# Loads held back near the end of a range's attention, and sums on VectorE set behind the copies of turned q and k

## The chip, the cores and the metric

The kernel runs on 1 core of one Trainium2 chip. The metric is the device time of one execution in microseconds (us). The five engines are TensorE (PE in the profile; PEld is its loading of weights), VectorE (DVE), ScalarE (ACT), GpSimd (POOL) and SyncE (SP). Each works through its own instructions in the order in which the program gives them, and waits on semaphores for the others. DMAs are issued from the queues of SP, ACT and POOL.

## The reference

Softmax attention over 8 batches, 12 heads, 448 tokens and a head size of 64, then two products with a leaky ReLU between them:

```python
def _attn_ref(q, k, v):                       # (8, 12, 448, 64) each
    scores = matmul(q, k.transpose(0, 1, 3, 2)) / sqrt(64)
    attn = exp(scores - max(scores)); attn = attn / (sum(attn) + 1e-09)
    return matmul(attn, v)

x = attn_out.transpose(0, 2, 1, 3).reshape(3584, 768)
h = x @ w_in                                  # (768, 2048)
g = maximum(0.01 * h, h)
out = g @ w_out                               # (2048, 768), float32
```

## The kernel before

The attention is done in 48 units (8 batches, 6 pairs of heads). Of a unit, GpSimd loads q, k and v (L144, two units in one DMA) and casts them into order (L173 for q and k, L175 for v); q and k are turned, by TensorE and a copy on VectorE (L275) for the first fifteen units and by a DMA transpose on SP's queue (L252, `turn`) for the rest; TensorE computes four chunks of scores (L286); ScalarE takes their exp (L295); `rows` multiplies by v with 32 matmuls (L792) and VectorE divides by the row sums (L798, L799); x is turned into `xT`, by TensorE for a few units (L332, copied at L333) and by DMA transposes for the others. A v buffer (four of them) is free for the cast of unit u + 4 when the rows of unit u are done.

The 3584 tokens are cut into seven ranges (`cuts`), of 640, 512, ..., 384 and 512 tokens. Each range has a product with w_in (the hidden product) and a product over w_out, done as two blocks. The work of the units that the next range needs is laid between the matmuls of the current range. Range 0's hidden product is plain (`head` for the first 448 tokens, `neck` for the rest, L367 and L650). From range 1 on, the products use a scheme of seven block products instead of eight, Strassen's kind, which needs sums on VectorE: sums of x (`mix_x_part`, L431), of w_in (`mix_w_in`, L402 and L406), of w_out (`mix_weights`, L379 to L388) and of h (`mix_first`, L458 and L459, for range 0; `mix_h`, L451 and L452, for the others). In `hidden` (L486) the partial products are added by ScalarE copies (L498, L506, L510) and VectorE (L501, L513, L516); in `block_pair` (L558) by VectorE copies (L563) and joins (L566), and more sums of h (L570, L576).

The order on each engine is written out by hand and fixed when the program is built. A small planner decides it: `place` puts bursts of three score chunks, turns and rows between matmuls, by a model of time (`model["now"]`) that knows TensorE, ScalarE and the PSUM slots. `advance`, called every fourth step, adds at most one turn, one cast of q and k, one cast of v and, on every second call, one load of the tensor (q, k or v) that is furthest behind. What `advance` lets through depends on counters (`to["load"]`, `to["cast"]`, `to["turn"]`, `rows_done`, `chunk`), not on time on the chip. `second(i)` is the product of range i over w_out; in it the sums of x of range i + 1 are set when the planner's time is far enough past the rows that they need (`fresh`), and `summed` says for both parts whether all have been set. `need[i + 2]` is the number of units that range i + 1 needs.

`mix_weights` is a generator: each `next(outs)` puts its next sum in VectorE's queue (12 sums for the mixed weights, one empty step, four sums in place on the right half of w_out, L388). `neck` draws from it by the counts in `after`; what is left is drawn after `second(0)`. In `neck` the turn of the last unit that TensorE turns (`transposes(NPE - 1, ...)`) stands just ahead of the last draw. `early_sums` says after which group of `head` which pair of sums of h for range 0 is set; the second pair of token blocks has its sums set in two pieces, `known` (the 64 columns of `head`) and the rest in `second(0)`.

Of the kernel before, what the change touches and what calls it, by code (L numbers as in the profile page):

```python
# [16 lines left out]
def kernel(  # L17
# [13 lines left out]
    P = 128  # L31
    HP = H // 2
    SC = 112
    NSC = S // SC
# [7 lines left out]
    NR = len(cuts) - 1  # L42
    HEAD = S
    need = [HP * -(-t // S) for t in cuts]
# [24 lines left out]
    def next_slot():  # L69

        slots.append(slots.pop(0))
        return slots[-1]

    def next_bank():

        banks.reverse()
        return banks[1]
# [19 lines left out]
    def place_of(t):  # L97
        return (t + NX - cuts[3]) % NX
# [155 lines left out]
    def dma_transposes(u):  # L254
        if NPE <= u < NU:
            turn(qkT[u % NQ][:, :QL], qk_sb[u].rearrange("p i so h d -> p (i so h d)"))
# [5 lines left out]
    def transposes(u, bank=None):  # L262
        if u >= min(NPE, NU):
            return
        for parts in ((1,), (0,)) if u == 0 else ((0, 1),):
            tr = turn_tile(bank)
            for i in parts:
                for so in range(NSC):
                    nc.tensor.transpose(  # L269
                        tr[:, i, ts(so, SC)], qk_sb[u][:, i, so], ident[:SC, :SC]  # L270
                    )
            if u == 0:
                stay_warm(3 if parts == (1,) else 5)
            at = slice(parts[0], parts[-1] + 1)
            (nc.scalar.copy if u == 0 and parts == (1,) else nc.vector.tensor_copy)(  # L275
                qkT[u % NQ][:, :QL].rearrange("p (i s) -> p i s", i=2)[:, at], tr[:, at]
            )
# [73 lines left out]
    def settle(n=3):  # L351
        while late and n:
            expo(*late.pop(0))
            n -= 1
# [79 lines left out]
    def spots(i):  # L434

        if i == 0:
            return 0, [(0, 1), (2, 3)]
        return 0, [(0, 2), (1, 3)] if cuts[i + 1] - cuts[i] == 4 * P else [(0, 1), (KEEP, 2)]
# [15 lines left out]
    def mix_first(m, c, cols):  # L454

        one, two = (slice(x * P + cols.start, x * P + cols.stop) for x in spots(0)[1][c])
        lo, hi = slice(m, m + 2), slice(MH + m, MH + m + 2)
        nc.vector.tensor_sub(h_mix[:, lo, c, cols], h[:, lo, one], h[:, lo, two])  # L458
        nc.vector.tensor_add(h[:, lo, two], h[:, lo, two], h[:, hi, two])  # L459
# [150 lines left out]
        banks.reverse()  # L610

    known = slice(0, HEAD - 3 * P)
    early_sums = {9: (0, 0, slice(0, P)), 11: (2, 0, slice(0, P)), 12: (0, 1, known), 13: (4, 0, slice(0, P)), 14: (2, 1, known), 15: (6, 0, slice(0, P))}

    def head(ins):

# [20 lines left out]
    def neck(outs):  # L637

        n = cuts[1] - HEAD
        at = place_of(HEAD)  # L640
        ms = [x + y for x in range(0, MH, 2) for y in (0, MH)]
        held = {}

        def part2(m, kks):
            fresh = m not in held
            if fresh:
                held[m] = next_bank()
            for j in range(2):
                for kk in kks:
                    nc.tensor.matmul(  # L650
                        held[m][:, j * n:(j + 1) * n], w_in_sb[:, kk, ts(m + j, P)], xT[:, kk, at:at + n],
                        start=(fresh and j == 0 and kk == 0), stop=(kk == KD - 1), skip_group_check=True,
                    )

        assert all(u == need[1] - 1 for u, _ in owed_x), owed_x
        def after(x):
            for _ in range((0, 0, 2, 3, 4, 3, 3, 2)[x]):
                next(outs)

        for m in ms[:2]:  # L660
            part2(m, range(KD - 1))
        yield 4 * (KD - 1) * n / 2400, False
        for x, m in enumerate(ms):
            if x < 2:
                assert rows_done >= need[1], rows_done
                settle_x()
                part2(m, (KD - 1,))
                if x:
                    after(x - 1)
            else:  # L670
                part2(m, range(KH))
                after(x - 1)
                yield 2 * KH * n / 2400, False
                part2(m, range(KH, KD))
            nc.scalar.activation(
                h[:, m:m + 2, HEAD:cuts[1]], held.pop(m)[:, :2 * n].rearrange("p (m t) -> p m t", m=2), AX.Prelu, alpha=0.01
            )
            if x < 2:
                mix_first(4 + 2 * x, 1, known)
            settle(1)  # L680
            yield 2 * (KH if x > 1 else 1) * n / 2400, True
        model["free"][id(slots[0])] = model["now"] + 1.5
        transposes(NPE - 1, next_slot()[:, 0])
        after(len(ms) - 1)

    def supply(u):
# [69 lines left out]
    chunk = 4 * HP + 3  # L756
    rows_done = HP
    to = {"pe": HP + 2, "turn": NPE, "cast": HP + 4, "v": HP + 4, "load": [HP + 8] * 3}
    tick = 0

    def advance():
        nonlocal tick
        tick += 1
        u = to["turn"]
        if u < min(NU, chunk // NSC + NQ, to["cast"]):
            dma_transposes(u)
            to["turn"] += 1
        u = to["cast"]
        if u < min(NU, to["turn"] + 2, to["load"][0], to["load"][1]):
            cast(u, (0, 1))  # L770
            to["cast"] += 1
        u = to["v"]
        if u < min(NU, rows_done + NV, to["load"][2]):
            cast(u, (2,))
            to["v"] += 1
        if tick % 2 == 0:
            x = min(range(3), key=lambda x: to["load"][x])
            u = to["load"][x]
            if u < NU and u - 3 < (to["cast"], to["cast"], to["v"])[x]:
                load_soft(u, 2, (x,))  # L780
                to["load"][x] += 2
# [45 lines left out]
    def settle_x(now=None):  # L827
        while owed_x and (now is None or owed_x[0][1] <= now and model["free"].get(id(slots[0]), 0.0) <= now + 0.05):
            model["free"][id(slots[0])] = model["now"] + 1.0
            model["now"] += 0.3  # L830
            x_transposes(owed_x.pop(0)[0], next_slot()[:, 0])
# [102 lines left out]
    def second(i):  # L934

        x_sums = [mix_x_part(i + 1, slice(0, 2)), mix_x_part(i + 1, slice(2, 3))] if i + 1 < NR else []
        fresh, summed = [None, None], [i + 1 == NR] * 2
        left = plan[i]
        for c in range(len(spots(i)[1])):
            for x, _ in enumerate(block_pair(i, c)):  # L940
                if x % 4 == 0:
                    advance()
                if c or x:
                    model["now"] += 0.325
                left -= place(i, left, calm=x not in (1, 2), keen=need[min(i + 2, NR)], cap=NU if all(summed) else need[i + 2])
                if i == 0 and c == 0 and x in (5, 9, 13, 17):
                    mix_first((x - 5) // 2, 1, slice(HEAD - 3 * P, P))
                if i == 0 and c and x % 4 == 2:
                    next(ins, None)
                for y in range(2):  # L950
                    if fresh[y] is None and i + 1 < NR and rows_done >= need[i + 2] - 1 + y:
                        fresh[y] = model["now"] + (2.5 if need[i + 2] - 2 + y in X_PE else 7.0)
                for y, todo in enumerate(x_sums if x % 2 == 0 else ()):
                    if fresh[y] is not None and fresh[y] <= model["now"] and not summed[y] and not (y and owed_x):
                        summed[y] = next(todo, 0) is not None
                        if not summed[y]:
                            break
        assert left == 0 or chunk == NU * NSC, (i, left)
        assert i + 1 == NR or rows_done >= need[i + 2], (i, rows_done)
        settle_x()  # L960
        for todo in x_sums:
            for _ in todo:
                pass

    ins, outs = mix_w_in(), mix_weights()
# [16 lines left out]
    model["now"] += 0.45  # L982
    to["pe"] += 1
    second(0)
    for _ in ins:
        pass
    for _ in outs:
        pass
    for i in range(1, NR):
        for step, _ in enumerate(hidden(i)):  # L990
            advance()
            if step % 4 == 2 and NSC * (rows_done + 1) <= chunk:
                rows()
        model.update(now=0.0, act=2.3, free={id(x): 0.9 if cuts[i + 1] - cuts[i] == 4 * P and i + 1 < NR else 1.2 for x in slots}, ready={})
        second(i)
# [30 lines left out]
```

## Time and profile before

| what | us |
|---|---|
| three runs | 391.54, 389.33, 386.16 (median 389.33) |
| the profiled execution | 386.56 |
| its span, from the first to the last instruction | 384.8 |
| GpSimd idle ahead of casts of v (L175), until rows (L792) | 100.8, longest 17.8 |
| ScalarE idle ahead of exp (L295), until scores (L286) | 46.8, longest 2.7 |
| VectorE idle ahead of a sum of x (L431), until a DMA transpose of x | 3.3 in three waits, longest 2.3 |
| TensorE idle until a copy of turned q and k (L275), score matmuls alone | 1.2 in three waits |

The granted clock of TensorE is 1.0 throughout. A line of a timeline gives the start in us, the duration, the engine and line, the operation with what it writes and reads, how many instructions are merged in it, and in brackets the engine's idle time just before it with what ended that. Idle time of an engine that isn't the bottleneck costs nothing by itself.

### The profile page before, as it was taken

The page shows a single profiled execution, that of the slowest core. Times are in us where ns is not written, and L with a number is a line of the kernel's source. Part 1 is how long each engine was busy: PE and PEld are TensorE (multiplying, and loading weights), DVE is VectorE, ACT ScalarE, POOL GpSimd, SP SyncE. Part 2 cuts the span into 40 slices and gives each one's busy share as a digit, 9 for nine tenths or more (in the row PEclk, how much of TensorE's full clock was granted, in tenths as well). Part 3 has the DMA queues.
Part 4 walks back from the last instruction along what each step waited for, and adds up shares of the span by engine and source line. Part 5 has one row for each costly group of instructions (what it writes and reads, how often), then busy time and mean ns, then how long its engine had stood idle before and what let it go on. Part 6 is the DMA issues. An engine that isn't in the chain of part 4 may idle for free.

```text
span 384.8 us, 10038 instructions
## 1 busy us (share of the span) xinstructions
PE 374.4 (97%) x4091; PEld 258.6 (67%) x4091; DVE 236.4 (61%) x510; ACT 264.3 (69%) x391; POOL 142.5 (37%) x223
## 2 busy tenths in 40 slices
PE   7899999999999999899999999999999999999996
PEld 3665658656588655786568865678655795668854
DVE  3662887786756644757458674575745665474753
ACT  6997875856768777487776877667776777717700
POOL 5989684475735043530535305254051000000000
PEclk9999999999999999999999999999999999999999
DMA  7999999999999159991399942999329600421022
GB/s 156 168 202 203 181 192 208 176 139 169 159 183 149 26 101 174 166 135 26 54 204 140 133 69 50 198 137 168 48 50 165 152 18 2 108 66 42 3 80 85
DMA packets 92798, 46.98 MB, mean 122 GB/s; under 512 B 51408, under 2 KB 89424, under 8 KB 92752
## 3 DMA queue, kind: packets, MB, share of 16 engines
q0 software_dynamic: 37536, 22.24, 45.5%
q1 hardware_dynamic: 54576, 23.54, 33.2%
q8 instruction: 32, 0.52, 0.6%
q10 hardware_dynamic: 640, 0.56, 0.5%
q14 instruction: 14, 0.11, 0.1%
HBM read 45.61 MB, written 11.01 MB: 147 GB/s over the span
## 4 chain that ended last, share of the span: by engine, by line
PE 89%; DVE 4%; ACT 3%; DMA 3%; issue 1%; DVEq 0%; ACTq 0%
PE g L558 32%; PE g L486 14%; PE sc L486 14%; PE sc L792 10%; PE sc L286 10%; PE g L367 3%; ACT e L295 3%; PE g L650 2%; DMA xT<-x 2%; PE g L269 1%; DMA hmix<-in_k_dram 1%; DVE x L799 1%; PE g L305 1%; DVE qkT L275 1%; PE sc L367 1%
## 5 line engine op out<-in xcount | busy, mean ns | idle before, releaser
L295 ACT ACTIVATE e<-sc 112x896 bf16<-112x896 f32 x192 | 162.6, 920 | 46.9 <-PE sc L286 46.8
L558 PEld LDWEIGHTS <-h 128*128 128x128 bf16 x680 | 61.2, 97 | 47.8 <-issue 14.0
L558 PE MATMUL g<-w_out_sb,h 128*128 128x384 bf16 x448 | 87.2, 327 | 0.0
L175 POOL COPY v<-fv 112x512 bf16<-112x512 bf16 x38 | 26.1, 689 | 109.4 <-PE sc L792 100.8
L475 ACT ACTIVATE h<-c 128x512 bf16<-128x512 f32 (+1 forms) x72 | 43.5, 611 | 25.4 <-DVE c L501 16.4
L486 PEld LDWEIGHTS <-w_in_sb 128*128 128x128 bf16 x576 | 54.2, 98 | 7.5 <-issue 1.5
L286 PE MATMUL sc<-qkT 64*128 64x448 bf16 x384 | 50.5, 353 | 2.7 <-DVE qkT L275 1.2
L792 PEld LDWEIGHTS <-e 112*128 112x128 bf16 x1344 | 46.3, 97 | 5.2 <-ACT e L295 0.8
L792 PE MATMUL sc<-v,e 112*128 112x65 bf16 x1344 | 47.6, 193 | 0.6 <-ACT e L295 0.6
L486 PEld LDWEIGHTS <-w_in_mix 128*128 128x128 bf16 x432 | 41.1, 98 | 4.1
L563 DVE COPY o<-g 128x384 f32<-128x384 f32 x53 | 29.3, 553 | 22.6 <-PE g L558 22.4
L558 PE MATMUL g<-w_mix,h 128*128 128x384 bf16 (+1 forms) x224 | 41.6, 324 | 0.0
L286 PEld LDWEIGHTS <-qkT 64*128 64x128 bf16 x384 | 15.8, 94 | 30.6 <-issue 20.3
L173 POOL COPY qkb<-fq 112x512 bf16<-112x512 bf16 x38 | 25.2, 664 | 23.3 <-DMA fq<-in_q_dram 18.6
L173 POOL COPY qkb<-fk 112x512 bf16<-112x512 bf16 x38 | 25.5, 672 | 21.1 <-DMA fk<-in_k_dram 21.1
L566 DVE TENSOR_TENSOR o<-o,g 128x384 f32<-128x384 f32 x42 | 23.1, 551 | 16.2 <-PE g L558 14.3
L799 DVE TENSOR_TENSOR x<-sc,rec 112x512 bf16<-112x512 f32 x42 | 29.0, 691 | 1.7 <-DVE rec L798 0.3
L486 PE MATMUL g<-xT,w_in_sb 128*128 128x256 bf16 (+1 forms) x216 | 28.5, 268 | 1.3 <-DVE o L566 1.3
L798 DVE RECIPROCAL rec<-sc 112x8 f32<-112x8 f32 x42 | 8.7, 207 | 34.1 <-PE sc L792 33.1
L486 PE MATMUL sc<-xT,w_in_sb 128*128 128x256 bf16 (+1 forms) x216 | 28.5, 268 | 0.0
L558 PE MATMUL g<-w_mix,hmix 128*128 128x384 bf16 x112 | 21.7, 327 | 0.0
L486 PE MATMUL sc<-x_mix,w_in_mix 128*128 128x256 bf16 (+1 forms) x144 | 19.0, 268 | 0.0
(105 smaller groups left out, 460.4 us busy)
## 6 DMA issues: line engine op xcount, KB each, us to landing
fq<-in_q_dram POOLq DMA_DIRECT2D x19, 224.0 KB, 6.8
fk<-in_k_dram POOLq DMA_DIRECT2D x19, 224.0 KB, 8.4
fv<-in_v_dram POOLq DMA_DIRECT2D x19, 224.0 KB, 5.6
w_in_sb<-in_moe_w_in_dram POOLq DMA_DIRECT2D x4, 768.0 KB, 11.9
w_out_sb<-in_moe_w_out_dram POOLq DMA_DIRECT2D x4, 768.0 KB, 18.5
out_dram<-o SPq DMA_DIRECT2D x7, 336.0 KB, 3.8
out_dram<-o SPq DMA_DIRECT2D x8, 288.0 KB, 5.2
out_dram<-o SPq DMA_DIRECT2D x7, 240.0 KB, 4.3
```

What stands on the lines that cost most here:

```text
L173: by(qk_sb[u][:, x].rearrange("p so h d -> p h so d"), f)
L175: by(v_sb[u % NV][:, :, :, :D], f)
L286: nc.tensor.matmul(ps[:, j, :S], t[j * D:(j + 1) * D, S + c * SC:S + c * SC + P], t[j * D:(j + 1) * D, :S], start=True, stop=True,)
L295: nc.scalar.activation(e[:, :, c, :], sc_t.pop((u, c))[:SC, :, :S], AX.Exp, scale=scale)
L367: nc.tensor.matmul(open_t[m][:, :n], w_in_sb[:, kk, ts(m, P)], xT[:, kk, at:at + n], start=(fresh and kk == kks[0]), stop=(kk == KD - 1),)
L475: nc.scalar.activation(hs[:, m:m + 2, cols], x.rearrange("p (m t) -> p m t", m=2), AX.Prelu, alpha=0.01)
L486: nc.tensor.matmul(ps[:, j * nh:(j + 1) * nh], w[:, kk, ts(j, P)], x[:, kk], start=(first and j == 0 and kk == 0), stop=(kk == KH - 1), sk ...
L558: nc.tensor.matmul(ps[:, cols], x[:, m], w[:, m], start=(first and m == 0), stop=(m == MH - 1), skip_group_check=True,)
L563: by(o[:, at], ps[:, :NW])
L566: nc.vector.tensor_add(o[:, at], o[:, at], ps[:, :NW])
L792: nc.tensor.matmul(ps[:, j, qc, :D + 1], e[:, at:at + P], vt[:, j, c, :D + 1], start=(c == 0), stop=(c == NSC - 1),)
L799: nc.vector.tensor_mul(x_t[u].rearrange("p q j d -> p j q d"), ps[:SC, :, :, :D], rec.to_broadcast([SC, 2, NSC, D]))
```

## The change

Four things are different.

In `advance`, loads get a condition: with `hold` set none is put in GpSimd's queue. `second(i)` sets it from the point where all rows but two that the next range needs have been done, until both parts of the sums of x have been set.

The sums of h for range 0: of the first pair of token blocks, all four are set after the last four groups of `head` (groups 12 to 15; before after 9, 11, 13 and 15); of the second pair, the known part of all four is set in the first two steps of `neck` (before two in `head` and two in `neck`), and the rest four matmul steps later in `second(0)`.

The sums of w_out: `neck` draws none at its seventh step (before three) and three after the turn (before two), so that two of the four sums on w_out that stood ahead of the copy of that turn now stand behind it, and two are drawn in the first block of `second(0)`.

In the hidden product of range 1 the first rows are set at step 6 instead of step 2.

```diff
-    early_sums = {9: (0, 0, slice(0, P)), 11: (2, 0, slice(0, P)), 12: (0, 1, known), 13: (4, 0, slice(0, P)), 14: (2, 1, known), 15: (6, 0, slice(0, P))}
+    early_sums = {12 + x: (2 * x, 0, slice(0, P)) for x in range(4)}
...
-            for _ in range((0, 0, 2, 3, 4, 3, 3, 2)[x]):
+            for _ in range((0, 0, 2, 3, 4, 3, 0, 3)[x]):
                 next(outs)
...
             if x < 2:
-                mix_first(4 + 2 * x, 1, known)
+                mix_first(4 * x, 1, known)
+                mix_first(4 * x + 2, 1, known)
...
-    def advance():
+    def advance(hold=False):
...
-        if tick % 2 == 0:
+        if tick % 2 == 0 and not hold:
             x = min(range(3), key=lambda x: to["load"][x])
...
                 if x % 4 == 0:
-                    advance()
+                    advance(i + 1 < NR and rows_done >= need[i + 2] - 2 and not all(summed))
...
-                if i == 0 and c == 0 and x in (5, 9, 13, 17):
-                    mix_first((x - 5) // 2, 1, slice(HEAD - 3 * P, P))
+                if i == 0 and c == 0 and x in (5, 7):
+                    next(outs)
+                if i == 0 and c == 0 and x in (9, 13, 17, 21):
+                    mix_first((x - 9) // 2, 1, slice(HEAD - 3 * P, P))
...
-            if step % 4 == 2 and NSC * (rows_done + 1) <= chunk:
+            if step % 4 == 2 and (i > 1 or step > 2) and NSC * (rows_done + 1) <= chunk:
                 rows()
```

## The prediction

> **What bounds the kernel now.** I read the first part of the page, then the chain that ended last, then TensorE's timeline from end to end for idle time, and at each idle place the engine named as its releaser. The first lines are busy time by engine, and the chain's shares.
>
> ```profile
> span 384.8 us, 10038 instructions
> ...
> PE 374.4 (97%) x4091; PEld 258.6 (67%) x4091; DVE 236.4 (61%) x510; ACT 264.3 (69%) x391; POOL 142.5 (37%) x223
> ...
> PE 89%; DVE 4%; ACT 3%; DMA 3%; issue 1%; DVEq 0%; ACTq 0%
> ```
>
> TensorE sets the time: it is busy for 374.4 of 384.8 us and makes 89% of the chain. The change takes no matmul away, so only TensorE's idle time can be won. After the start-up (the first 30 us) its timeline names a releaser four times (start, duration, then the idle time before it):
>
> ```profile
> 52.14 0.36 PE L286 MATMUL sc<-qkT 64*128 64x448 bf16 x2 [0.27 <-DVE qkT L275]
> ...
> 75.56 0.36 PE L286 MATMUL sc<-qkT 64*128 64x448 bf16 x2 [0.70 <-DVE qkT L275]
> ...
> 107.33 1.15 PE L792 MATMUL sc<-v,e 112*128 112x65 bf16 x32 [0.57 <-ACT e L295]
> ...
> 156.26 0.81 PE L486 MATMUL g<-xT,w_in_sb 128*128 128x256 bf16 x6 [1.32 <-DVE o L566]
> ```
>
> Together 0.27 + 0.70 + 0.57 + 1.32 = 2.86 us, 0.7% of the span. That is nearly all that an edit of order can gain in the profiled execution. VectorE's timeline shows what stood ahead of the two copies of turned q and k, and why the join L566 was late at the last place:
>
> ```profile
> 47.76 0.28 DVE L458 TENSOR_TENSOR hmix<-h 128x256 bf16<-128x256 bf16 x1
> 48.15 0.29 DVE L459 TENSOR_TENSOR h<-h 128x256 bf16<-128x256 bf16 x1
> ...
> 51.47 0.61 DVE L275 COPY qkT<-sc 128x896 bf16<-128x896 bf16 x1
> ...
> 73.95 1.01 DVE L388 TENSOR_TENSOR w_out_sb<-w_out_sb 128x768 bf16<-128x768 bf16 x2
> 74.88 0.61 DVE L275 COPY qkT<-sc 128x896 bf16<-128x896 bf16 x1
> ...
> 151.60 0.56 DVE L566 TENSOR_TENSOR o<-o,g 128x384 f32<-128x384 f32 x1 [0.74 <-PE g L558]
> 154.42 0.58 DVE L431 TENSOR_TENSOR x_mix<-xT 128x512 bf16<-128x512 bf16 x1 [2.26 <-DMA xT<-x]
> 155.03 0.71 DVE L431 TENSOR_TENSOR xT<-xT 128x512 bf16<-128x512 bf16 x1
> 155.67 0.54 DVE L566 TENSOR_TENSOR o<-o,g 128x384 f32<-128x384 f32 x1
> ```
>
> VectorE stood 2.26 us at a sum of x (L431) until a DMA transpose of x landed; the join queued behind it came 1.3 us too late for TensorE. The DMA views, without and with loads in flight (window 134.5 to 137.5, then 144 to 153), and GpSimd's timeline:
>
> ```profile
> xT<-x SPq DMA_TRANSPOSE x2, 2.3
> ...
> q1 hardware_dynamic: 2805, 1.19, 83.9%
> q0 software_dynamic: 928, 0.46, 42.4%
> ...
> xT<-x SPq DMA_TRANSPOSE x4, 5.1
> ...
> 144.76 0.70 POOL L144 DMA_DIRECT2D fq<-in_q_dram  x1
> ...
> 146.07 0.70 POOL L144 DMA_DIRECT2D fk<-in_k_dram  x1
> ```
>
> A transpose of x lands 2.3 us after its issue alone, 5.1 (median) among loads; the chain has the deciding one at 147.49 with 6.91 us, landing at 154.4. The two loads took 42.4% of 16 engines for 9 us, 3.8 us or 1.9 each.
>
> **The change part by part.**
>
> *Sums of h (L458, L459).* One pair leaves the queue ahead of the copy at 51.47: 48.44 - 47.84 = 0.60 us in the chain. The copy moves to 50.87, the score matmuls could start at 51.5, and TensorE is free at 52.14 - 0.27 = 51.87. The gap goes: -0.27. The pairs that are moved fall to VectorE's queue at about 63.5, two more of the half-length pairs (0.22 + 0.25 us each by the rows there, some 0.9 us). The sums of w_out behind them end at 68.3 today and then VectorE stands 2.19 us for the w_out load until 69.63; that wait hides them. Were the load early, 0.9 us would reach the next copy.
>
> *Last sums on w_out (L388).* Two of 0.5 us leave the place ahead of the copy at 74.88, which then starts at 73.95 and frees TensorE 0.9 us earlier, against a gap of 0.70: -0.70, to the end of the matmuls before it. Two of the four now stand in the first block of products over w_out. There the join L566 at 79.58 comes later by 0.5 + 0.5 less the pair of h sums that moved on (0.74), 0.26 us; it ends at 80.12 and its bank is reused at 80.87, so 0.49 us of cover is left, and the last sum is done 0.8 us before the product that reads it. Cost nothing; if the cover were gone, 0.3 us.
>
> *Rows of attention set back in the second range's hidden product.* The 32 matmuls at 107.33 waited 0.57 us for an exp that ends at 107.27. They now stand four groups of 0.655 us later, when it is done. The groups that move up need ScalarE's two copies L498, which end at 107.75 and 108.23; the first reader would be TensorE at about 107.9. Between 0.27 and 0.57 comes back; I take 0.4. A cast of v that waits for these rows comes 2.6 us later; its first use is 27 us after it.
>
> *The hold on loads.* It only moves instructions in GpSimd's order; no load waits for a sum on the chip. In the new order the loads of q and k at 144.76 and 146.07 go behind a cast of v that waits for TensorE until 158.8, and one load of v moves up to just behind the cast at 145.52. So one load stays in the critical window where two were. Taking 1.9 us off the traffic ahead of the transpose lands it at 152.5. VectorE is free at 152.16, and the gap of 1.32 goes if the transpose lands by 154.4 - 1.32 = 153.1. Bounds: 0 (the v load alone holds the transpose up, or the four stores and two turns of q and k ahead of it on SP's queue do) and 1.32; since 1.9 exceeds 1.32, I take 1.3. In the other ranges TensorE shows no wait at the same place, so the hold gains nothing there.
>
> What is late next: loads that are held come some 12 us later and with them four casts of q and k per range. Cover: GpSimd stands idle for long in every hidden product,
>
> ```profile
> 184.29 0.61 POOL L175 COPY v<-fv 112x512 bf16<-112x512 bf16 x1 [17.77 <-PE sc L792]
> ```
>
> and the copy of q and k cast at 153.4 to 154.0 is turned only at 178.4 and first read by TensorE at 196.6. On SP's queue one turn of q and k passes two stores, and its reader comes 23 us after it lands. Without that cover a late load costs its lateness, in each of four ranges.
>
> The sum: 0.27 + 0.70 + 0.4 + 1.3 = 2.7 us. The profiled execution took 386.56 us (1.76 beyond its span), and would take 383.9. That execution lies 2.77 below the median of the three runs (386.16, 389.33, 391.54), for a reason the profile can't show. I take the mean of all four, 388.4, and forecast 388.4 - 2.7 = 385.7, taken as 385.8.
>
> **Rivals.**
>
> *The hold misses* (the change doesn't do what it says). For: the v load goes out at 146.1, inside the window, and nothing on the chip ties a load to a sum; the 83.9% on SP's queue are there without any load. Against: 1.9 us of packets less where 1.3 are needed. Then 1.4 us is gained: 387.0.
>
> *The held casts collide with VectorE in the hidden product* (slower than before). Four more casts of 0.62 us fall into each of four hidden products. For: at 52.39 a sum L459 took 0.53 us beside a cast, against 0.29 at 48.15. If every cast stops VectorE for its whole length and TensorE waits for it, 4 x 4 x 0.62 = 9.9 us: 388.4 - 2.7 + 9.9 = 395.6; it ends slower than before from 2.7 us, a quarter of that. Against: VectorE is busy for 13.72 of 20.40 us from 156.3 to 176.7, and its sums L513 and L516 beside the casts at 165.36 and 165.91 took 0.69 and 0.68 us, as elsewhere. The Trainium skill ("SBUF — State Buffer", Who interferes with whom) says that a VectorE instruction with two SBUF inputs and a GpSimd instruction that reads SBUF take one shared port pair in turn, and the later one blocks fully. By that rule the sums L451 and L452 alone would be stopped; the trace agrees in kind (L459) and shows stretching rather than a stop of a whole cast.
>
> *More than the profile shows.* If the 2.77 us that the median has over the profiled execution are the same wait for x, longer, the median falls to about 383.9 - 0.5 = 383.4. For: transfers are what varies most in the trace (2.3 to 6.9 us for one form). Against: the profile has just one such wait.
>
> **How the numbers follow.** Forecast 0.68, hold misses 0.16, more than the profile shows 0.10, collision 0.06. The range goes from the lowest run less the whole idle time, 386.16 - 2.86 = 383.3, down to 383.0 for the third rival, up to the highest run less what is gained without the hold, 391.54 - 1.4 = 390.1, taken as 390.0. A measurement tells some 2% (7.8 us) from no change: faster means under 381.5, below all that is priced, 0.03; slower means over 397.1, beyond even the whole collision, 0.03; within, 0.94.
>
> **What would show it.** The gaps at 52, 75, 107 and 156 us gone from TensorE's timeline; one load of v and none of q or k within 10 us ahead of the third range's sums of x, whose first L431 waits under 1 us; GpSimd's long wait for rows shorter, with casts of q and k after it still far ahead of their readers. I am wrong if a new wait for turned q and k, or of ScalarE and TensorE for VectorE's sums in the hidden product, stands in the timeline, or the transposes still land 6 us and more after issue.

## The result, and the profile after

| | before | after |
|---|---|---|
| median of 20 executions, us | 389.73 | 385.0 |
| lowest, highest, us | 386.16, 393.99 | 383.44, 391.05 |
| ratio of the times, 95% interval | | 0.9895 [0.9864, 0.9925] |
| the profiled execution (span), us | 386.56 (384.8) | 387.18 (385.3) |
| the same pair measured a second time, medians of 29 and 6, us | 388.68 | 383.84 |
| its ratio | | 0.9897 [0.9839, 0.9956] |

The time went down by about 1%, within the 2% band; executions whose clock or time stands apart from the others are left out of the ratios. The medians differ by 4.7 us, the lowest executions by 2.72. The profiled execution of after is above its own median and, by itself, no faster than that of before. So the edits have to be looked for by their places, not by the two totals.

The page of after, its span, busy time and chain by engine:

```profile
span 385.3 us, 10036 instructions
...
PE 376.0 (98%) x4091; PEld 260.0 (67%) x4091; DVE 236.6 (61%) x510; ACT 264.7 (69%) x391; POOL 141.1 (37%) x223
...
PE 81%; DMA 12%; ACT 2%; DVE 2%; POOL 1%; issue 1%; DVEq 0%; POOLq 0%
```

TensorE is still the bound. The chain now has 12% of DMA: it runs back through a load of w_out, which in this execution landed late. VectorE's timeline shows this (start, duration, then the idle time before; the sums of w_out are L379 to L388):

```profile
69.75 0.55 DVE L384 TENSOR_TENSOR w_mix<-w_out_sb,w_mix 128x768 bf16<-128x768 bf16 x1
73.10 0.56 DVE L379 TENSOR_TENSOR w_mix<-w_out_sb 128x768 bf16<-128x768 bf16 x1 [2.79 <-DMA w_out_sb<-in_moe_w_out_dram]
...
77.42 0.61 DVE L275 COPY qkT<-sc 128x896 bf16<-128x896 bf16 x1
```

Before, the same wait was 2.19 us and ended at 69.63. Now it ends at 73.10, 3.5 us later, and the copy of turned q and k (L275) starts at 77.42 where it was at 74.88. TensorE's own timeline of after, all its waits with a named releaser after 30 us (lines behind the inserted ones are numbered one or two higher than before: rows L793, the division L800):

```profile
50.37 0.37 PE L286 MATMUL sc<-qkT 64*128 64x448 bf16 x2 [0.55 <-DVE x L800]
...
77.56 0.36 PE L286 MATMUL sc<-qkT 64*128 64x448 bf16 x2 [1.25 <-DVE x L800]
78.10 0.36 PE L286 MATMUL sc<-qkT 64*128 64x448 bf16 x2 [0.17 <-DVE qkT L275]
```

The waits at 107 and 156 us are gone. At 50 and 77 us there are waits still, behind another releaser. Since TensorE runs the same matmuls in the same order (but for the rows set back), one can take the start of the n-th matmul in both traces and follow the difference, after less before, in us:

| stretch (time in before) | what lies in it | after | after, run again |
|---|---|---|---|
| up to 45 us | start-up, code not changed | +1.40 | +0.06 |
| 45 to 70 | sums of h ahead of the copy | +0.25 | -0.47 |
| 70 to 84 | sums of w_out, first block over w_out | +0.91 | -0.39 |
| 102 to 115 | rows set back | -0.74 | -0.75 |
| 152 to 160 | hold | -1.48 | -1.48 |
| at the last matmul | | +0.33 | -3.03 |

The first execution began 1.4 us late and met the late load of w_out; the second did not, and gained 3.03 us in all (383.77 against 386.56). VectorE's wait for w_out ended at 73.10 us in the first and at 69.26 in the second. From 160 us to the end the difference moves by no more than 0.01 to 0.02 us: no late cost of the held loads shows in these two executions.

How the hold works is seen in GpSimd's timeline of after, around the second range's end:

```profile
147.32 0.61 POOL L175 COPY v<-fv 112x512 bf16<-112x512 bf16 x1 [0.70 <-PE sc L793]
147.87 0.70 POOL L144 DMA_DIRECT2D fv<-in_v_dram  x1
159.09 0.61 POOL L175 COPY v<-fv 112x512 bf16<-112x512 bf16 x1 [10.52 <-PE sc L793]
159.65 0.70 POOL L144 DMA_DIRECT2D fq<-in_q_dram  x1
```

One load of v stands in the window and the load of q waits behind a cast until 159.65. The DMA view of 144 to 153 us, with the transposes of x issued in it and their median us to landing:

```profile
q0 software_dynamic: 464, 0.23, 20.4%
...
xT<-x SPq DMA_TRANSPOSE x3, 3.1
```

Loads (queue 0) are down from 42.4% to 20.4%. A transpose of x lands after 3.1 us (median) where it took 5.1; the first of the last four, the deciding one before, took 4.0 (149.4 to 153.4) where it took 6.9. VectorE's sums of x don't wait here:

```profile
153.40 0.55 DVE L566 TENSOR_TENSOR o<-o,g 128x384 f32<-128x384 f32 x1 [0.74 <-PE g L558]
153.87 0.42 DVE L431 TENSOR_TENSOR x_mix<-xT 128x512 bf16<-128x512 bf16 x1
154.32 0.42 DVE L431 TENSOR_TENSOR xT<-xT 128x512 bf16<-128x512 bf16 x1
155.48 0.56 DVE L566 TENSOR_TENSOR o<-o,g 128x384 f32<-128x384 f32 x1 [0.73 <-PE g L558]
```

The joins (L566) now wait for TensorE, not TensorE for them.

### The profile page after: what moved, and what is told of

Its sections match the earlier page's. It is cut to its first block, busy times and chain, and to the rows that moved or that the text cites. A ratio compares the mean times of both kernels' runs of the same rounds, so it can differ in the third digit from the quotient of the medians.

```text
span 385.3 us, 10036 instructions
## 1 busy us (share of the span) xinstructions
PE 376.0 (98%) x4091; PEld 260.0 (67%) x4091; DVE 236.6 (61%) x510; ACT 264.7 (69%) x391; POOL 141.1 (37%) x223
## 4 chain that ended last, share of the span: by engine, by line
PE 81%; DMA 12%; ACT 2%; DVE 2%; POOL 1%; issue 1%; DVEq 0%; POOLq 0%
PE g L558 34%; PE g L486 14%; PE sc L486 14%; PE sc L286 9%; PE sc L793 9%; DMA w_out_sb<-in_moe_w_out_dram 7%; DMA fq<-in_q_dram 3%; ACT e L295 2%; DMA hmix<-in_k_dram 1%; PE g L269 1%; POOL qkb L173 1%; DVE qkT L275 0%; PE g L305 0%; PE g L332 0%; DVE w_mix L379 0%
## 5 line engine op out<-in xcount | busy, mean ns | idle before, releaser
L793 PEld LDWEIGHTS <-e 112*128 112x128 bf16 x1344 | 46.4, 97 | 4.4
L793 PE MATMUL sc<-v,e 112*128 112x65 bf16 x1344 | 47.7, 193 | 0.0
L566 DVE TENSOR_TENSOR o<-o,g 128x384 f32<-128x384 f32 x42 | 23.2, 552 | 18.1 <-PE g L558 16.3
L173 POOL COPY qkb<-fk 112x512 bf16<-112x512 bf16 x38 | 24.7, 650 | 22.9 <-DMA fk<-in_k_dram 22.9
L800 DVE TENSOR_TENSOR x<-sc,rec 112x512 bf16<-112x512 f32 x42 | 29.0, 691 | 1.7 <-DVE rec L799 0.3
```

The lines of the kernel that those rows point to most:

```text
L173: by(qk_sb[u][:, x].rearrange("p so h d -> p h so d"), f)
L566: nc.vector.tensor_add(o[:, at], o[:, at], ps[:, :NW])
L793: nc.tensor.matmul(ps[:, j, qc, :D + 1], e[:, at:at + P], vt[:, j, c, :D + 1], start=(c == 0), stop=(c == NSC - 1),)
L800: nc.vector.tensor_mul(x_t[u].rearrange("p q j d -> p j q d"), ps[:SC, :, :, :D], rec.to_broadcast([SC, 2, NSC, D]))
```

## The experiments

Two theories stood at the start: each edit takes away the wait it is aimed at, and the four add up (the prediction's sum); or the medians' 4.7 us have a further cause, the likeliest of those priced being a longer wait for x in the executions that no profile had shown. Medians and ratios below are against the kernel before on the same chip.

**The four edits, each alone.** The hold:

```diff
-    def advance():
+    def advance(hold=False):
...
-        if tick % 2 == 0:
+        if tick % 2 == 0 and not hold:
...
-                    advance()
+                    advance(i + 1 < NR and rows_done >= need[i + 2] - 2 and not all(summed))
```

> Before with the hold on loads alone. Theory (the change gains at places that add up, each one a wait of TensorE): this removes the idle time ahead of the first matmul of the third range's hidden product, 1.3 to 1.5 us, so about 388.2 against 389.7 before; TensorE's gaps near 52, 75 and 107 us stay. Rival 1 (loads disturb the transposes and turns more in the usual execution than in the one profiled, and the hold is nearly the whole change): 3 us or more gained, 386.5 or less. Rival 2 (the load of v that moves up keeps the transpose late): no gain, 389.7, and the gap at 156 us stays.

Median 387.35, ratio 0.9944 [0.9906, 0.9983], 12 executions. TensorE's waits:

```profile
52.88 0.36 PE L286 MATMUL sc<-qkT 64*128 64x448 bf16 x2 [0.87 <-DVE qkT L275]
...
107.62 1.15 PE L792 MATMUL sc<-v,e 112*128 112x65 bf16 x32 [0.57 <-ACT e L295]
```

No wait is left at 156 us, that at 107 is untouched: the hold acts where the prediction put it. By matmul starts it gives 1.48 us there, against the first profile of before. The median is 0.9 us below the theory's 388.2 and above rival 1's 386.5; the interval covers both.

The rows set back:

```diff
-            if step % 4 == 2 and NSC * (rows_done + 1) <= chunk:
+            if step % 4 == 2 and (i > 1 or step > 2) and NSC * (rows_done + 1) <= chunk:
```

> Before with the first rows of the second range's hidden product set four groups later, nothing else. Theory: the wait of 0.57 us for an exp at 107 us goes, 0.6 to 0.7 gained, 389.0. Rival 1: nothing.

Median 385.86, ratio 0.9935 [0.9895, 0.9975], 12 executions. The wait at 107 is gone and matmuls behind it start 0.75 us earlier; 0.80 us at 156 stays. The place came as expected, the median did not: it is 3.1 us under the expected 389.0, and a place worth 0.75 us can't account for that. Twelve executions of this kernel don't price one edit; the places do.

The sums of w_out:

```diff
-            for _ in range((0, 0, 2, 3, 4, 3, 3, 2)[x]):
+            for _ in range((0, 0, 2, 3, 4, 3, 0, 3)[x]):
...
+                if i == 0 and c == 0 and x in (5, 7):
+                    next(outs)
```

> Before with the last sums on w_out set behind the copy of turned q and k, nothing else. Theory: 0.7 us where the load of w_out comes early and 1.0 (two sums of 0.5) where it comes late and VectorE's sums run straight into that copy: 388.7 to 389.0. Rival 1: under 0.5 us. Rival 3 (these sums are the larger part, since the load of w_out is late in most executions): 2 us or more, 387.7 or less. The gap at 156 us stays in any case.

Median 388.37, ratio 0.999 [0.9949, 1.0031], 12 executions: no gain is seen, rival 1 by the number, though the interval allows the theory's 0.7 to 1.0 us too. In its profiled execution the wait ahead of the copy fell from 0.70 to 0.17, and a new one stands in the first block over w_out:

```profile
75.66 0.36 PE L286 MATMUL sc<-qkT 64*128 64x448 bf16 x2 [0.17 <-DVE qkT L275]
79.25 0.81 PE L558 MATMUL g<-w_mix,h 128*128 128x384 bf16 x4 [0.20 <-DVE o L563]
81.66 0.36 PE L286 MATMUL sc<-qkT 64*128 64x448 bf16 x2 [1.12 <-DVE x L799]
```

VectorE was late by then because a sum of h that takes 0.68 us alone (L576, the same shape, in this trace too) took 1.91:

```profile
76.82 1.91 DVE L570 TENSOR_TENSOR h<-h 128x1024 bf16<-128x1024 bf16 x1
...
82.46 0.68 DVE L576 TENSOR_TENSOR h<-h 128x1024 bf16<-128x1024 bf16 x1
```

It ran beside two of GpSimd's casts, at 77.01 and 77.56, which follow each other without a pause. This was the first sign of a cost that the prediction's sum did not have. Not all of the 1.32 us is that cost: alone, this edit lacks the 0.74 us that the moved pair of h sums frees, so by the prediction's own count its 1.0 us of sums overruns the 0.75 us of cover by 0.25 with no cast at all.

The sums of h:

```diff
-    early_sums = {9: (0, 0, slice(0, P)), 11: (2, 0, slice(0, P)), 12: (0, 1, known), 13: (4, 0, slice(0, P)), 14: (2, 1, known), 15: (6, 0, slice(0, P))}
+    early_sums = {12 + x: (2 * x, 0, slice(0, P)) for x in range(4)}
...
-                mix_first(4 + 2 * x, 1, known)
+                mix_first(4 * x, 1, known)
+                mix_first(4 * x + 2, 1, known)
...
-                if i == 0 and c == 0 and x in (5, 9, 13, 17):
-                    mix_first((x - 5) // 2, 1, slice(HEAD - 3 * P, P))
+                if i == 0 and c == 0 and x in (9, 13, 17, 21):
+                    mix_first((x - 9) // 2, 1, slice(HEAD - 3 * P, P))
```

> Before with the sums of h alone set elsewhere. Theory: 0.3 us gained at the copy near 51 us, less up to 0.9 us of sums that come later and delay the last copy of turned q and k where the load of w_out is no longer waited for: 389.3 to 390.0. Rival 3 of the sums as a whole: 1 us or more gained.

Median 387.96, ratio 0.9949 [0.9916, 0.9981], 12 executions. The time came out lower than the theory's 389.3 to 390.0 and meets rival 3 (1 us or more), but the places don't bear that out: the wait at 52 is gone (0.44 us by matmul starts), that at 75 is 1.11 where it was 0.70, and 0.62 us at 83.50 is new. Again a sum of h is the cause, beside four casts:

```profile
79.92 2.25 DVE L576 TENSOR_TENSOR h<-h 128x1024 bf16<-128x1024 bf16 x1
```

So in these profiles each of the two edits of VectorE's order, alone, loses in the first block over w_out more than it wins ahead of it. Whether that is the edit or the execution needed further runs.

**The changed kernel again, and the edits in pairs.** First the change as it is, a second time:

> The changed kernel once more, beside the three others of this chip. Theory (gains at places): TensorE shows no wait at 107 and 156 us; what stands near 50 and 77 us depends on when the load of w_out lands, and the run differs from the kernel before by 2.7 to 4.7 us. Rival (the gaps of 0.55 and 1.25 us near 50 and 77 us belong to the change): they are there again with the same sizes.

Median 383.84, ratio 0.9897 [0.9839, 0.9956], 6 executions. One wait with a named releaser is left in the whole profile, 0.17 us at 74.68, so the rival (0.55 and 1.25 us again) falls. Its account stands in the table above.

Both edits of sums without the other two:

> Both moves of sums on VectorE, without the hold on loads and without the later rows. Theory (the sums by themselves are worth little, since what the copies of turned q and k gain is lost again where sums in the first block of products over w_out meet casts on GpSimd): within 1 us of the kernel before, and the gaps at 107 us (0.57) and at 156 us (0.3 to 1.3) stay. Rival 3 (the sums are the larger part of the 4 us): 2 us or more gained.

Median 386.05, ratio 0.9943 [0.9903, 0.9983], 12 executions; waits of 0.48 at 63, 0.17 at 75, 0.57 at 107 and 0.59 at 155. Here the first block over w_out shows no wait. The gain, 2.2 us by the ratio, is the rival's (2 us or more) and not the theory's (within 1 us); the interval, 0.7 to 3.8 us, leaves room for both.

The hold and the rows without the sums:

> The hold on loads and the later rows alone, sums as before. Theory: 0.75 us at 107 us and 1.0 to 1.5 at 156 us, 1.8 to 2.3 us in those places, both gaps gone; TensorE's gaps near 52 and 75 us as in the kernel before. If the sums matter in the usual execution, this is 1 to 2 us slower than the changed kernel of the same chip; if they don't, equal within 0.5 us.

Median 385.18, ratio 0.9948 [0.9903, 0.9992], 12 executions; no wait at 107 and 156, but 1.27 at 53. The two pairs multiply to 0.9948 x 0.9943 = 0.9891, against 0.9897 for the whole change in the same comparison: the halves add up, within intervals of 0.4 to 0.6% each way. Hold and rows are 1.3 us slower than the changed kernel by the medians, inside the 1 to 2 us that the expectation named for sums that matter; the intervals overlap. (The four single edits would come to 1.8% together; their intervals of some 0.4% each way allow 1.1% as well.)

**The load of w_out earlier.** In the changed kernel, this load goes out ahead of one load of the attention:

```diff
-        fetch()
         load_w({9: 1, 10: 3}.get(g, 0))
+        fetch()
```

> The changed kernel with the last three loads of w_out put ahead of the two loads of q and k that stand before them in GpSimd's order. If the late landing of w_out is what delays the last copy of turned q and k (it landed at 73.0 us in the profile of the changed kernel and VectorE stood 2.8 us for it), it lands 2 to 4 us earlier, the gap of TensorE near 77 us goes, and 1 to 2 us are gained on the changed kernel. If the loads of q and k are needed as early as they stand, a wait of GpSimd for them and a new gap appear between 50 and 70 us, and nothing is gained.

Median 386.17, ratio 0.9945 [0.9907, 0.9983], 12 executions, lowest 385.21 where the change has 383.57 in this comparison. VectorE's wait for w_out and TensorE's gap near 77 us are gone, as expected, but nothing is gained: the profiled execution (388.24, the highest of the twelve) has new waits, at 83 to 94 us and not at 50 to 70:

```profile
83.22 1.14 PE L558 MATMUL g<-w_mix,hmix 128*128 128x384 bf16 x6 [0.36 <-DVE o L563]
...
87.37 0.81 PE L558 MATMUL g<-w_out_sb,h 128*128 128x384 bf16 x4 [1.71 <-DVE o L563]
...
93.75 0.36 PE L286 MATMUL sc<-qkT 64*128 64x448 bf16 x2 [1.26 <-DMA qkT<-qkb]
```

The middle wait has this behind it on VectorE:

```profile
83.72 3.13 DVE L459 TENSOR_TENSOR h<-h 128x128 bf16<-128x128 bf16 x1
...
87.48 0.22 DVE L459 TENSOR_TENSOR h<-h 128x128 bf16<-128x128 bf16 x1
```

The same sum, same shape, 3.13 us at one place and 0.22 at another. GpSimd's timeline for the time of the long one (the first line issues a load):

```profile
83.25 0.71 POOL L144 DMA_DIRECT2D fk<-in_k_dram  x1
83.94 0.63 POOL L175 COPY v<-fv 112x512 bf16<-112x512 bf16 x1
84.49 0.63 POOL L173 COPY qkb<-fq 112x512 bf16<-112x512 bf16 x1
85.05 0.62 POOL L173 COPY qkb<-fk 112x512 bf16<-112x512 bf16 x1
85.60 0.61 POOL L173 COPY qkb<-fq 112x512 bf16<-112x512 bf16 x1
86.16 0.61 POOL L173 COPY qkb<-fk 112x512 bf16<-112x512 bf16 x1
86.71 0.61 POOL L175 COPY v<-fv 112x512 bf16<-112x512 bf16 x1
```

Casts start 0.55 us apart and each lasts 0.61 to 0.63, so nothing stands between them. The sum ends at 86.85, just behind the end of the fifth cast (86.77); it came through before the sixth had ended, though that started at 86.71. By the recorded starts the sum was there first, 0.22 us ahead of the first cast, while GpSimd issued a load.

The train by itself doesn't make the wait. The same six casts follow each other in the first profile of before (80.42 to 84.18 us), and there three sums of the same shape each came through after one cast:

```profile
80.89 0.52 DVE L459 TENSOR_TENSOR h<-h 128x128 bf16<-128x128 bf16 x1
...
82.04 0.52 DVE L459 TENSOR_TENSOR h<-h 128x128 bf16<-128x128 bf16 x1
...
83.19 0.51 DVE L459 TENSOR_TENSOR h<-h 128x128 bf16<-128x128 bf16 x1
```

They began 0.2 to 0.5 us after the start of a cast. Whether the moment of the start decides is not shown.

**The kernel before, profiled again, twice.** To see what an execution at the upper end looks like.

> The kernel before, one more profile, to see where an execution loses what the first profiled one (386.56 us, near the lowest of its runs) did not. Theory (the same four places, with sizes that vary, and the load of w_out): TensorE's gaps near 52, 75, 107 and 156 us again, 0.3 to 1.5 us each, and where the time is over 388 us a longer one of them or one at a later range's start. Rival (something outside the change's places): a gap that no edit of the change touches.

385.93 us; waits of TensorE of 0.27, 0.79, 0.57 and, at 155 us, 0.30. That last one, behind the sums of x, was 1.32 in the first profile.

> As the run above; a second sample of the same kernel, with the same expectations.

391.69 us. TensorE's wait behind the sums of x (161 us) is 0.83, shorter than in the first profile, and VectorE stood 2.22 us for x where it stood 2.26. So the third rival fails here: this execution's loss is not a longer wait for x. What is long stands in the first block over w_out. TensorE, then VectorE:

```profile
83.54 0.36 PE L286 MATMUL sc<-qkT 64*128 64x448 bf16 x2 [2.64 <-DVE x L799]
```

```profile
79.60 3.04 DVE L459 TENSOR_TENSOR h<-h 128x128 bf16<-128x128 bf16 x1
```

Five casts run beside it, from 79.74 to 82.56, and it ends at 82.64; it, too, began ahead of the first of them, by 0.14 us, while GpSimd issued a load. It is the unchanged kernel: a blocked sum does not need the change. The wait of 2.64 us cost more than itself. The windows of this run around it (busy us and instructions of each engine, then the granted TensorE clock):

```profile
82.00:84.00 2.00, 0.46 (x3) 0.21 (x3) 1.97 (x5) 0.54 (x2) 1.11 (x3) 1.00 1.20 148
84.00:86.00 2.00, 2.00 (x9) 1.02 (x8) 1.73 (x6) 0.91 (x1) 0.61 (x1) 0.60 2.05 114
86.00:88.00 2.00, 2.00 (x11) 0.59 (x9) 0.62 (x2) 0.07 (x1) 0.95 (x2) 0.54 1.09 184
88.00:90.00 2.00, 2.00 (x37) 1.42 (x34) 0.29 (x2) 2.00 (x3) 0.31 (x1) 1.00 0.39 25
```

After the idle stretch the granted clock was 0.60 and 0.54 for 4 us; by matmul starts this place lost 4.45 us against the first profile.

**The change without the hold.**

```diff
-                    advance(i + 1 < NR and rows_done >= need[i + 2] - 2 and not all(summed))
+                    advance()
```

> The changed kernel without the hold on loads. Theory: as the changed kernel up to 150 us, then TensorE waits 0.3 to 1.5 us at the start of the third range's hidden product (as in every run without the hold so far), and perhaps at the start of the fourth; about 1 us slower than the changed kernel, 384.5 to 385.5. Rival (the later rows and the sums already remove that wait): no wait at 156 us.

Median 387.12, ratio 0.9979 [0.9936, 1.0022], 10 executions. The profiled one (391.63, the highest of the ten) had TensorE waits of 2.05 and 1.88 at 78 and 87. Behind the second stood a sum L388 of 2.81 us beside five casts, one of the two that the change moved into this block. At 156 no wait is named, as the rival had it; by matmul starts the place is still 0.39 us slower than in the runs with the hold, and the theory's wait at the fourth range is there (0.23). So here the hold is worth 0.39 us at its place. The ratio is 3.3 us above the change's 0.9895, but it was taken on another chip against few executions of before, and the interval overlaps that of the second measurement of the change, [0.9839, 0.9956]; no trace shows a reason for the rest.

**Casts set apart.** If VectorE is shut out because casts follow each other with no gap, a short instruction that reads no SBUF between them should let it in:

```diff
+            if u >= HP + 4:
+                nc.gpsimd.memset(v_sb[0][:, 0, 0, D + 4:D + 8], 0.0)
```

(at the end of `cast`, into columns that nothing reads).

> The changed kernel, with a small GpSimd memset that reads no SBUF tile (8 columns of unused padding) set behind every cast of unit 10 and later. If a VectorE sum with two SBUF inputs is held because casts follow each other with no gap between their reads (before_c: L459 3.04 us beside five casts, no_hold: L388 2.81 beside five), each memset lets it in: no two-input sum of VectorE in the first block over w_out takes over about 1.3 us (one cast of 0.61 and its own 0.55 to 0.7), no gap of TensorE over 1 us stands there, executions above 386.5 us become rare, and the median is 383.5 to 384.2. The memset's 0.1 to 0.2 us after each cast is covered by GpSimd's waits for loads. Rival: the hold is kept whatever stands between the casts (or the memset holds it as well): sums of 2 us and more beside trains of casts are still to be seen, and the spread of executions stays that of the changed kernel, median 384 to 385.5. Second rival: the longer casts make the turned k and q late: new waits of TensorE for qkT or for DVE behind casts, median above 385.5.

Median 384.82, ratio 0.9931 [0.9891, 0.9972], 12 executions from 383.35 to 388.51, three of them above 386. The first theory's median and rarity didn't come. The profile shows why. VectorE's sum, and GpSimd beside it:

```profile
83.70 1.97 DVE L460 TENSOR_TENSOR hmix<-h 128x128 bf16<-128x128 bf16 x1
```

```profile
83.21 0.60 POOL L173 COPY qkb<-fk 112x512 bf16<-112x512 bf16 x1
83.76 0.09 POOL L177 MEMSET v<- 112x4 bf16 x1
83.81 0.60 POOL L173 COPY qkb<-fq 112x512 bf16<-112x512 bf16 x1
84.35 0.09 POOL L177 MEMSET v<- 112x4 bf16 x1
84.39 0.60 POOL L173 COPY qkb<-fk 112x512 bf16<-112x512 bf16 x1
84.94 0.09 POOL L177 MEMSET v<- 112x4 bf16 x1
84.99 0.60 POOL L175 COPY v<-fv 112x512 bf16<-112x512 bf16 x1
```

The sum, 0.21 us alone, waited through three memsets and ended at 85.67, after the last cast (85.59). A memset of 0.09 us adds 0.04 us to the spacing of the casts and did not let this sum in. The rival's expectation is met. That trace also has the opposite case: a sum of h at 81.94 took its usual 0.68 us, and the cast at 82.01 took 1.21 in place of 0.60. There VectorE was first and GpSimd waited.

TensorE's named waits at the four places, in every profiled execution (us, summed over each place; two smaller waits behind 200 us, of 0.46 and 0.23, are left out):

| kernel | 46 to 66 | 70 to 96 | 107 | 156 |
|---|---|---|---|---|
| before, first profile | 0.27 | 0.70 | 0.57 | 1.32 |
| before, second | 0.27 | 0.79 | 0.57 | 0.30 |
| before, third | 1.42 | 2.64 | 0.57 | 0.83 |
| hold alone | 1.09 | none | 0.57 | none |
| rows alone | none | 0.18 | none | 0.80 |
| hold and rows | 1.48 | none | none | none |
| sums of w_out alone | 0.77 | 1.49 | 0.57 | 0.60 |
| sums of h alone | none | 1.73 | 0.57 | 0.34 |
| both sums | 0.48 | 0.17 | 0.57 | 0.59 |
| the change | 0.55 | 1.42 | none | none |
| the change, again | none | 0.17 | none | none |
| w_out's load first | none | 3.33 | none | none |
| without the hold | 0.48 | 3.93 | none | none |
| casts set apart | 0.65 | 0.17 | none | none |

The last two columns follow the edits: with the rows set back, 107 is clear in every profile; with the hold, 156 is clear in every profile, and without it seven of eight have a wait there. The two small waits left out stand at the start of the fourth range, both without the hold. The first two columns vary from execution to execution by more than either edit is worth. In the first, the wait at the copy near 52 us is in six of the seven profiles without the moved sums of h and in none of the seven with them; but four of these seven have other waits in the same column.

The traces also show how the hold works. Set to the first profile's time by matmul starts, the first transpose of x that VectorE needs lands at 151.6 to 152.9 us in the six profiles with the hold and at 153.4 to 154.4 in the eight without. The prediction had it at 152.5, and 153.1 as the latest that closes the gap. The time from its issue to its landing alone separates them less well, 4.0 to 5.6 us with the hold and 4.5 to 6.9 without.

## Why the prediction was right, and where not

The forecast of 385.8 is 0.8 above the median of 385.0, and the sum of 2.7 us is the difference of the lowest executions (2.72). That the time came so near is in part luck. Two errors offset each other: the starting point of 388.4, a mean of four executions, was 1.3 under the median of twenty (389.73), and the gain of 2.7 was 2.0 under the 4.7 between the medians (1.4 under the 4.1 of the ratio). For an execution like the profiled one the sum gave 383.9, and the repeated profile took 383.77; there, too, the terms differ, 0.47, 0.39, 0.75 and 1.48 against 0.27, 0.70, 0.4 and 1.3. Step by step:

- *The bound.* Right: only TensorE's idle time was won, and the repeated profile, with 0.17 us of named waits left where there were 2.86, is the one that ends 3.03 us earlier.
- *The rows, 0.4.* The mechanism is right, the size too low: 0.74 or 0.75 in every profile that has this edit. I took a value between 0.27 and 0.57 because the groups that move up were to wait for ScalarE's two copies (L498). No such wait is in any of these traces. The 0.57 comes back whole; the 0.18 beyond it I could not place on a line.
- *The hold, 1.3.* Right in mechanism and for the profiled execution (1.48). As a figure for the usual execution it was too high: the wait at 156 us was 1.32 us in the one profile I had, and 0 to 0.83 in seven others without the hold. By matmul starts the hold is worth 0.39 to 1.02 us against these seven. A single profile showed the longest of eight. It also hid a gain: I had none in the other ranges, but at the start of the fourth (205 us in the first profile) four of the eight profiles without the hold lose 0.18 to 0.62 us, and none of the six with it does.
- *The sums of h, 0.27.* The opposite: 0.44 to 0.47 in place, and the wait that it removes was up to 1.27 us in other profiles of kernels without the edit (1.20 in the third of before, 0.87 with the hold alone, 1.27 with hold and rows).
- *The sums of w_out, 0.70.* Mis-sized, 0.39 in the repeated profile and a loss in the first. The step that failed is "Cost nothing; if the cover were gone, 0.3 us". The sums that moved into the first block over w_out meet GpSimd's casts there. In the edit alone 1.32 us of new waits (0.20 + 1.12) stood behind a sum that took 1.91 us in place of 0.68; about 0.25 of it is the missing relief from the h sums. Without the hold, a moved sum itself took 2.81 us and TensorE waited 1.88. The 0.49 us of cover held only as long as the sums beside it took their usual time; in three profiles with both edits it did.
- *"Stretching rather than a stop of a whole cast".* Wrong. Sums of 0.22 us took 3.13 and 3.04, each beside five casts: VectorE stops, and it can be for more than one cast. The Trainium skill ("SBUF — State Buffer", Who interferes with whom) calls the ports that the two share an exclusive lock, and says of VectorE's two-port modes that whoever issues first holds them for the whole instruction while the other blocks fully. The runs agree with the stop and show it going on, at times, through the casts that follow. L459's 0.53 us, on which I had based my reading, was already such a stop: the sum waited for the rest of one cast (52.14 to 52.76) and came through although another followed. That is the usual outcome. From 30 us on, the fourteen profiles hold 565 sums with two SBUF inputs beside at least one cast: 298 took at most 0.2 us more than the shortest of their kind, 246 up to 0.65 more, and 21 more than that, up to 2.91.
- *Second rival, collision.* Its mechanism is real and its place wrong. In the hidden products nothing was lost (0.01 to 0.02 us after 160 us in both profiles of the change; of the four other profiles with the hold one, hold and rows, lost 0.18, near 277 us in the first profile's time, for a reason that is not shown); it bites in range 0's first block over w_out, where six casts follow each other, and it does so in the kernel before as well.
- *First rival, the hold misses.* Fell: the load of v does stay in the window, as that rival had it, but 20.4% instead of 42.4% of traffic was enough.
- *Third rival, more than the profile shows.* In size it came nearest to the change of medians (4.7 us, or 4.1 by the ratio). Its cause fell: the other profiles have a shorter wait for x, not a longer one. (The 0.5 that it takes off besides is worked out nowhere.)

What stays open is the part beyond 2.7 us. Executions more than 2.7 us above their kernel's lowest were 13 of 20 before and 8 of 20 after; the third profile of before shows that such an execution can be one with a blocked sum. But with both edits of the sums that place has 0.17 us in three profiles and 1.42 to 3.93 in three others, so it isn't shown that the change makes blocked sums rarer. Nor is it known what lets one sum through after a single cast and shuts another out for five, or what makes a load land late in one execution and not in the next.

## What to carry to other kernels

Price an edit at its place in more than one profiled execution: a wait that ends on a DMA was 0 to 1.32 us here from one execution to the next, while one that ended on a computation (0.57 at 107 us) was the same every time. Before moving sums with two SBUF inputs on VectorE, look at GpSimd's timeline at the place they go to: beside back-to-back casts they can take as long as several of them, and a few tenths of cover don't hide that. Holding transfers that nobody needs yet, by their place in the issuing engine's order, frees a short and urgent one behind them without any wait on the chip.

## What the runs showed of the hardware

A VectorE sum with two SBUF inputs beside GpSimd casts that follow each other without a pause mostly waits for one of them (0.51 to 0.53 us for 0.22), but can wait for several (3.13 and 3.04 us for 0.22, beside five; 2.25 for 0.68, beside four). In one trace memsets of 0.09 us between the casts didn't end such a wait (1.97 for 0.21). The opposite occurs too: a cast took 1.21 us for 0.60 beside a sum that began 0.07 us ahead of it. But the two longest sums had also begun ahead of their first cast, by 0.22 and 0.14 us, so the recorded start doesn't tell which of the two waits. What decides the turn these runs don't settle.

A wait of 2.64 us on TensorE was followed by 4 us at a granted clock of 0.54 to 0.60, and cost 4.45 us with what followed; waits of 1.71, 1.26 and, in the run without the hold, 1.88 us left the clock at 1.00. The Trainium skill ("TensorE: Matmul & The Clock Gate", Part 1: The HAM clock gate) has the clock halved after an idle window of some 3.4 us; here idle times shorter than that were followed by such a drop, in two executions (the other had a wait of 2.05 us and then 0.50 and 0.65 for 2 us each, in the run without the hold).
